# Top-k attention with an MLP behind it on one core: the opening loads, the place of the scores and the spread of the weight pieces

## The chip, the cores and the metric

The kernel runs on one core of a Trainium2 chip. The core has a matrix engine (TensorE, "PE" in the profile; its weight loads are "PEld"), a vector engine (VectorE, "DVE"), an engine for activations (ScalarE, "ACT"), a general one (GpSimd, "POOL") and one that issues transfers (SyncE, "SP"). Each works through its own list of instructions in order and waits on semaphores for the others. The metric is the device time of one execution in microseconds (us), the median over several.

## The reference

What is computed, with 8 batches, 8 heads, 576 rows and heads of 64, and then an MLP from 512 to 2048 and back:

```python
scores = (1 / sqrt(64)) * q @ k.T                  # per batch and head, 576 x 576
kth    = the 32nd largest score of each row
attn   = exp(scores - max), where scores >= kth, else 0
attn   = attn / (sum(attn) + 1e-9)
x      = (attn @ v), heads side by side            # 4608 x 512
h      = x @ w_in                                  # 4608 x 2048
out    = (h * sigmoid(1.702 * h)) @ w_out          # 4608 x 512
```

All data is float32.

## The kernel before

**Tiles and slots.** Heads are taken in pairs, four pairs a batch. The 576 rows of a head are four tiles of 128 rows and an end of 64. A *slot* is one tile of rows for one pair (two heads, 128 x 576 scores each), or the ends of two pairs. There are 144 slots, 18 a batch; slots 0 to 3 are the first row tile of the four pairs of batch 0.

**What a slot goes through.** `load` brings q and k of a pair (two transfers of 128 KB each and one of 32 KB for the 64 end rows), with row 4p + t on partition p at place t. `prepare` turns them on TensorE, and ScalarE copies the result to SBUF (L201, L206, L208). `scores` multiplies (L231), and ScalarE copies the scores out (L238). `topk` finds the 32 largest of each row on VectorE: eight MAX8 (L247) and six MATCH_REPLACE8 (L250), fourteen operations in a fixed order. `bounds` (GpSimd, L266, L267) takes the 32nd and the largest, `exponentials` (ScalarE, L275 a Prelu, L277 the exponentials with their sums) makes the unnormalised weights. `divide` inverts the sums on VectorE (L286, L288) and, in slots below SETTLED = 9, makes a diagonal matrix of them on GpSimd (L292), by which `turn` transposes and divides in one matmul (L308, L311); later slots divide on ScalarE and GpSimd (L294, L295). `values` multiplies by v (L338) into xT (L350). Once the four pairs of a row tile are there, `hidden` (L381), `tanh` (L398), `gate` (L411, L412, L414) and `project` (L429) do the MLP on it in four parts.

**Weights in pieces.** w_in and w_out are brought in 32 pieces of 128 x 512 float32 outputs, from raw transfers of 512 KB (L122), and `round_piece` splits the work on each: "size" on ScalarE (L144), "shift" on VectorE (L145), "low" and "sign" on ScalarE (L147, L146), "finish", two operations on GpSimd (L140, L141). `by_slot` says how many pieces each of slots 0 to 9 handles; the transfers of slot n's pieces are queued in slot n - 1, and eight raw buffers exist, each free when its piece is finished.

**The order.** It is written out by hand, in the order of the calls: `opening`, then `slot(n)` for n = 0 to 9, then `two_slots(n)`, which interleaves two slots. Every engine keeps this order. In `slot(n)` come the exponentials of slot n - 1, sizes, the preparing and scoring of slot n + 2, the top-k of slot n with the division of n - 1 after its sixth operation (i == 5), the shifts, and then turning and values of n - 1. Finishes not yet done wait in the list `unfinished`; a slot issues one after the third operation of its top-k and the others behind the division. `stay_warm` puts matmuls without a use on TensorE.

**Buffers and queues.** q and k of a pair lie in two buffers each, so pair 2 takes those of pair 0 once pair 0 has been turned. Scores have three buffers and the PSUM tiles for turning two. All transfers are issued by SP, in order; the order of the issues waits, for each transfer, for the one eight places before it, since eight completion semaphores go round.

Of the kernel before, what the change touches and what calls it, by code (L numbers as in the profile page):

```python
# [16 lines left out]
P = 128  # L17
# [11 lines left out]
def kernel(  # L29
# [6 lines left out]
    moe_w_out: bass.AP,  # L36
    out: bass.AP,
):

# [119 lines left out]
    def load(name, b, hp):  # L164
        src = q if name == "q" else k
        t = loads.tile([P, NF, 2, D], F32, name=f"{name}_l")
        for j in range(2):
            nc.sync.dma_start(t[:, :, j, :], src[b, 2 * hp + j, 0:FULL, :].rearrange("(p t) d -> p t d", t=NF))

        if name == "q":  # L170
            loaded["ends", b, hp] = loads.tile([P, 2, D], F32, name="ends")
        on = slice(0, TAIL) if name == "q" else slice(TAIL, P)
        nc.sync.dma_start(
            loaded["ends", b, hp][on, :, :], src[b, 2 * hp : 2 * hp + 2, FULL:S, :].rearrange("h p d -> p h d")
        )
        loaded[name, b, hp] = t

    def load_v(b, hp):
        main = vals.tile([P, 2, NF, D], F32, name="v_l")
        nc.sync.dma_start(  # L180
            main[:].rearrange("p j t d -> p j (t d)"),
            v[b, 2 * hp : 2 * hp + 2, 0:FULL, :].rearrange("j (p t) d -> p j (t d)", t=NF),
        )


        tail = v_ends[(b * NP + hp) % len(v_ends)]
        for j in range(2):
            nc.sync.dma_start(tail[j * TAIL : (j + 1) * TAIL, j, :], v[b, 2 * hp + j, FULL:S, :])
        vv[b, hp] = main, tail
# [138 lines left out]
    def values(n):  # L328
        b, t, hps = slots[n]
        pt = st[n]["pt"]  # L330
        outs = []
        for p in range(2 if t == NF else 1):
            cols = slice(p * TAIL, (p + 1) * TAIL) if t == NF else slice(0, P)
            main, tail = vv[b, hps[p]]
            o = ps_t.tile([P, 512], F32, name="o", tag="tp")
            for c in range(NF + 1):
                for j in range(2):
                    nc.tensor.matmul(  # L338
                        o[j * D : (j + 1) * D, 0 : cols.stop - cols.start],
                        lhsT=main[:, j, c, :] if c < NF else tail[:, j, :],  # L340
                        rhs=pt[:, j * NF + c if c < NF else 2 * NF, cols],
                        start=(c == 0),
                        stop=(c == NF),
                    )
            outs.append((o, hps[p]))
        for o, hp in outs:
            if t < NF:
                if (b, t) not in xts:
                    xts[b, t] = xtp.tile([P, CC, P], F32, name="xT")
                nc.scalar.copy(out=xts[b, t][:, hp, :], in_=o[:, 0:P])  # L350
            else:
                if (b // 2, t) not in xts:
                    xts[b // 2, t] = xtt.tile([P, CC, P], F32, name="xT_t")
                at = b % 2 * TAIL
                nc.scalar.copy(out=xts[b // 2, t][:, hp, at : at + TAIL], in_=o[:, 0:TAIL])
        if hps[-1] == NP - 1:
            if t < NF:
                to = out[b * S : b * S + FULL, :].rearrange("(p t) c -> p t c", t=NF)[:, t, :]
                ready.append((xts.pop((b, t)), [(slice(0, P), to)]))
            elif b % 2:  # L360
                first = [(b - 1 + i) * S + FULL for i in range(2)]
                rows = [(slice(i * TAIL, (i + 1) * TAIL), out[x : x + TAIL, :]) for i, x in enumerate(first)]
                ready.append((xts.pop((b // 2, t)), rows))
        st[n].clear()

# [53 lines left out]
    def project(blocks):  # L419
# [12 lines left out]
        if blocks[-1] == G - 1 and g == NG - 1:  # L432
            ob = osp.tile([P, C], F32, name="ob")
            nc.scalar.mul(out=ob[:], in_=po[:], mul=0.5 / RAISE**2)
            for on, to in rows:
                nc.sync.dma_start(to, ob[on, :])


    later = {}
# [7 lines left out]
    READY = (((-9, -8), (-7, -6), (-4, -3), (-2, -1)), ((-7, -6), (-4, -3), (-3, -2), (-1, -2)))  # L447
    FETCH = (((-13, -12), (-11, -10), (-7, -7), (-5, -4)), ((-11, -10), (-9, -8), (-5, -5), (-2, -2)))
    VALUES = ((-8, -7, 0, 0), (-8, -7, 2, 2))
    by_slot = dict(enumerate([2, 2, 3, 3, 3, 3, 4, 4, 4, 4]))  # L450
    for n in by_slot:
        first = sum(map(len, list(by_slot.values())[:n]))
        by_slot[n] = list(range(first, first + by_slot[n]))
    assert by_slot[len(by_slot) - 1][-1] == NPIECE - 1
    for n in range(2, len(by_slot)):
        for x in by_slot[n]:
            at(n - 1, load_piece, x)
        if n < NP + 1:
            at(n - 1, load_v, 0, n - 1)
    for hp in range(2, NP):  # L460
        for name in "qk":
            at(hp - 2, prepare, name, 0, hp)
    for b in range(1, B):
        for hp in range(NP):
            for i, name in enumerate("qk"):
# [2 lines left out]
            at(b * PER + VALUES[b % 2][hp], load_v, b, hp)  # L468
    unfinished = []

    early = []

    def opening():

        stay_warm(7, v_ends[0][:].rearrange("p j d -> p (j d)"))
        for hp in range(2):
            for name in "qk":
                load(name, 0, hp)
        for x in by_slot[0]:
            load_piece(x)  # L480
        for m in range(2):
            for name in "qk":
                prepare(name, 0, m)
            if m == 1:
                early.extend(round_piece(x) for x in by_slot[0])
                for piece in early:
                    piece["size"]()
            scores(m)
        for hp in range(2, NP):
            for name in "qk":  # L490
                load(name, 0, hp)
        load_v(0, 0)
        for x in by_slot[1]:
            load_piece(x)

    def slot(n):
        todo = later.pop(n, [])
# [7 lines left out]
        if before:  # L505
            bounds(n - 1)
            exponentials(n - 1)
        some = [round_piece(x) for x in by_slot.get(n, [])] if n else early
        if n == 0:
            for piece in some:  # L510
                piece["low"]()
                piece["sign"]()
        else:
            for piece in some[:2]:
                piece["size"]()
        if not settled:
            for args in preparing:
                prepare(*args)
            scores(n + 2)
            stay_warm(4)  # L520
        if n > 0:
            for piece in some[2:]:
                piece["size"]()
        tanh(aside)
        for i, op in enumerate(topk(n) if n < N else [lambda: None] * 14):
            op()
# [8 lines left out]
                gate(aside)  # L535
        for piece in some:
            piece["shift"]()
            unfinished.append(piece["finish"])
        if n == 0:
            return  # L540
        if aside:
# [1 line left out]
        if settled:  # L543
            for args in preparing[:1]:
                prepare(*args)
        for piece in some[:2]:
            piece["low"]()
        going = settled and len(to_project) > (2 if n < N else 0)
        if going:
            project(range(G - 1))  # L550
# [3 lines left out]
            project(range(G - 1, G))  # L554
        if before:
            turn_ends(n - 1)
        for piece in some[2:]:
            piece["low"]()
        if before:
            values(n - 1)  # L560
        for piece in some:
            piece["sign"]()
        if settled and n + 2 < N:
            scores(n + 2)
        if settled:
            for args in preparing[1:]:
                prepare(*args)
        if not ready and not settled:
            stay_warm(4)
        hidden()  # L570

    def two_slots(n):

# [23 lines left out]
        def find(m):  # L597
            for i, op in enumerate(topk(m) if live(m) else [lambda: None] * 14):
                op()
                if i == 5 and live(m - 1):  # L600
                    divide(m - 1)
                if i > 1 and unfinished:
                    unfinished.pop(0)()

        def middle(m):
# [74 lines left out]
```

## Time and profile before

| | before |
|---|---|
| time, median of 3 (lowest to highest) | 1630.75 us (1627.81 to 1632.36) |
| span of the profiled execution | 1630.6 us |
| TensorE busy | 1584.6 us, 97% |
| VectorE busy | 1479.2 us, 91% |
| ScalarE busy | 1155.9 us, 71% |
| GpSimd busy | 754.1 us, 46% |
| moved by DMA | 56.61 MB, mean 35 GB/s |

Busy shares are means over stages that differ: the first slots, in which the weights are still coming, have their own shares, and so has the end, where only the MLP is left. A row in order of time has its start, its length, the engine, the line, the operation with out<-in and, in square brackets, how long the engine stood idle before it and what ended that. A row "x3" merges three instructions, and its length is from the first one's start to the last one's end.

### The profile page before, as it was taken

The page shows a single profiled execution, that of the slowest core. Times are in us where ns is not written, and L with a number is a line of the kernel's source. Part 1 is how long each engine was busy: PE and PEld are TensorE (multiplying, and loading weights), DVE is VectorE, ACT ScalarE, POOL GpSimd, SP SyncE. Part 2 cuts the span into 40 slices and gives each one's busy share as a digit, 9 for nine tenths or more (in the row PEclk, how much of TensorE's full clock was granted, in tenths as well). Part 3 has the DMA queues.
Part 4 walks back from the last instruction along what each step waited for, and adds up shares of the span by engine and source line. Part 5 has one row for each costly group of instructions (what it writes and reads, how often), then busy time and mean ns, then how long its engine had stood idle before and what let it go on. Part 6 is the DMA issues. An engine that isn't in the chain of part 4 may idle for free.

```text
span 1630.6 us, 32137 instructions
## 1 busy us (share of the span) xinstructions
PE 1584.6 (97%) x12025; PEld 1184.1 (73%) x12025; DVE 1479.2 (91%) x3212; ACT 1155.9 (71%) x2449; POOL 754.1 (46%) x782
## 2 busy tenths in 40 slices
PE   7777999999999999999999999999999999999999
PEld 5665677777777777777777777777777777777776
DVE  6998999999999999999999998999999999999960
ACT  5896777777777776677777777777777777777761
POOL 2788344444444444444444444444444444444430
PEclk7898999999999999999999999999999999999999
DMA  7442001110001001110000100111000100000000
GB/s 209 124 137 76 22 22 29 30 43 16 22 15 44 22 23 29 29 37 22 22 15 23 35 17 15 30 30 44 15 22 15 43 22 23 22 8 7 8 8 14
DMA packets 100636, 56.61 MB, mean 35 GB/s; under 512 B 83584, under 2 KB 91776, under 8 KB 100480
## 3 DMA queue, kind: packets, MB, share of 16 engines
q1 hardware_dynamic: 100480, 54.55, 12.1%
q8 instruction: 95, 1.56, 0.4%
q14 instruction: 61, 0.50, 0.1%
HBM read 45.09 MB, written 9.44 MB: 33 GB/s over the span
## 4 chain that ended last, share of the span: by engine, by line
PE 88%; ACT 5%; DVE 4%; POOL 1%; issue 1%; SPq 0%; DMA 0%; POOLq 0%; ACTq 0%
PE ph L381 30%; PE po L429 29%; PE o L338 9%; PE s_ps L231 9%; PE tp L306 8%; DVE top L247 2%; DVE left L250 2%; PE tp L199 1%; ACT sc L238 1%; ACT pr L277 1%; ACT raw L146 1%; PE tp L308 1%; DVE wout L145 0%; ACT sc L275 0%; DMA raw<-in_moe_w_in_dram 0%
## 5 line engine op out<-in xcount | busy, mean ns | idle before, releaser
L247 DVE MAX8 top<-left 128x8 f32<-128x576 f32 x864 | 609.9, 747 | 0.0
L429 PE MATMUL po<-wout,gT 128*128 128x512 f32 x1152 | 542.1, 594 | 0.0
L381 PEld LDWEIGHTS ph<-xT,win 128*128 128x128 f32 x4096 | 467.5, 192 | 41.5 <-issue 40.8
L381 PE MATMUL ph<-xT,win 128*128 128x128 f32 x4096 | 484.6, 277 | 0.0
L250 DVE MATCH_REPLACE8 left<-top,left 128x576 f32<-128x576 f32 x576 | 423.4, 743 | 0.0
L295 POOL TENSOR_SCALAR pr<-pr,rden 128x576 f32<-128x576 f32 x135 | 233.4, 1729 | 356.0 <-ACT th L398 347.9
L411 POOL TENSOR_SCALAR th<-th 128x512 f32<-128x512 f32 x133 | 198.9, 1496 | 224.2 <-ACT th L398 224.2
L429 PEld LDWEIGHTS po<-wout,gT 128*128 128x128 f32 x1152 | 197.8, 191 | 142.3 <-issue 141.8
L275 ACT ACTIVATE sc<-sc,cut 128x576 f32<-128x576 f32 x288 | 208.1, 774 | 130.5 <-POOL cut L266 128.1
L316 ACT COPY pt<-tp 128x512 f32<-128x512 f32 (+1 forms) x432 | 193.2, 481 | 148.1 <-PE tp L306 141.0
L306 PEld LDWEIGHTS tp<-ident,pr 128*128 128x128 f32 x1215 | 145.7, 141 | 113.9 <-issue 65.8
L238 ACT COPY sc<-s_ps 128x576 f32<-128x576 f32 x288 | 169.9, 644 | 75.8 <-PE s_ps L231 75.4
L277 ACT ACTIVATE pr<-sc,low 128x576 f32<-128x576 f32 x288 | 219.2, 764 | 0.0
L247 DVE MAX8 top<-sc 128x8 f32<-128x576 f32 x288 | 202.2, 744 | 11.3 <-ACT sc L238 11.3
L250 DVE MATCH_REPLACE8 left<-top,sc 128x576 f32<-128x576 f32 x288 | 211.7, 743 | 0.0
L306 PE MATMUL tp<-ident,pr 128*128 128x128 f32 x1215 | 177.7, 273 | 9.0 <-ACT q_t L201 7.7
L231 PE MATMUL s_ps<-k_t,q_t 64*128 64x288 f32 (+1 forms) x1280 | 183.3, 433 | 0.9 <-ACT k_t L201 0.9
L412 POOL TENSOR_TENSOR gT<-th,h 128x512 f32<-128x512 f32 x133 | 169.8, 1277 | 11.1
L338 PE MATMUL o<-pt,v_l 128*64 128x128 f32 (+1 forms) x2560 | 158.9, 267 | 1.2 <-ACT pt L316 0.3
L338 PEld LDWEIGHTS o<-pt,v_l 128*64 128x64 f32 x2560 | 131.6, 138 | 31.3 <-ACT pt L316 15.8
L231 PEld LDWEIGHTS s_ps<-k_t,q_t 64*128 64x128 f32 (+1 forms) x1280 | 100.0, 178 | 59.6 <-issue 40.5
L266 POOL TENSOR_SCALAR cut<-top 128x2 f32<-128x2 f32 x144 | 38.2, 265 | 208.5 <-DVE top L247 206.8
(55 smaller groups left out, 1175.3 us busy)
## 6 DMA issues: line engine op xcount, KB each, us to landing
q_l<-in_q_dram SPq DMA_DIRECT2D x64, 128.0 KB, 2.9
k_l<-in_k_dram SPq DMA_DIRECT2D x64, 128.0 KB, 2.9
raw<-in_moe_w_in_dram SPq DMA_DIRECT2D x16, 512.0 KB, 5.1
v_l<-in_v_dram SPq DMA_DIRECT2D x32, 256.0 KB, 3.0
raw<-in_moe_w_out_dram SPq DMA_DIRECT2D x16, 512.0 KB, 3.3
out_dram<-ob SPq DMA_DIRECT2D x32, 256.0 KB, 2.3
ends<-in_q_dram SPq DMA_DIRECT2D x32, 32.0 KB, 2.4
ends<-in_k_dram SPq DMA_DIRECT2D x32, 32.0 KB, 2.6
```

What stands on the lines that cost most here:

```text
L231: nc.tensor.matmul(ps[i][rows, c, 0:HALF], lhsT=qT[b, hps[p]][on, cols], rhs=kT[b, hps[p]][on, FIRST[i] + c * HALF : FIRST[i] + (c + 1) * ...
L247: nc.vector.max(top[:, i, 8 * r : 8 * r + 8], (left if r else sc)[:, i, :])
L250: nc.vector.match_replace(left[:, i, :], top[:, i, 8 * r : 8 * r + 8], (left if r else sc)[:, i, :], LOWEST)
L275: nc.scalar.activation(sc[:, i, :], sc[:, i, :], AF.Prelu, bias=cut[:, i : i + 1], alpha=HUGE)
L277: nc.scalar.activation(pr[:, i * S : (i + 1) * S], sc[:, i, :], AF.Exp, bias=low[:, i : i + 1], accum_out=den[:, i : i + 1],)
L295: nc.gpsimd.tensor_scalar(pr[:, S : 2 * S], pr[:, S : 2 * S], rden[:, 1:2], None, op0=ALU.mult)
L306: nc.tensor.transpose(tp[:, c * P : (c + 1) * P], pr[:, at], ident[:])
L316: nc.scalar.copy(out=to, in_=tp[:, 0 : blocks * P])
L338: nc.tensor.matmul(o[j * D : (j + 1) * D, 0 : cols.stop - cols.start], lhsT=main[:, j, c, :] if c < NF else tail[:, j, :], rhs=pt[:, j * N ...
L381: nc.tensor.matmul(ph[:, i, :], lhsT=win[:, c, f * P : (f + 1) * P], rhs=xT[:, c, :], start=(c == 0), stop=(c == CC - 1),)
L411: nc.gpsimd.tensor_scalar(th[:], th[:], 1.0, None, op0=ALU.add)
L429: nc.tensor.matmul(po[:], lhsT=gT[:, i, :], rhs=wout[:, f, :], start=(f == 0), stop=(f == FC - 1))
```

## The change

It has five parts.

1. *First pair.* `load_first` issues k of pair 0 from ScalarE's queue, and only the first 128 rows of q (both heads, 64 KB) with the ends from SP. `prepare_first` turns these, with the small copies on VectorE. The other 384 rows of q are loaded behind pair 1 and the first two weight pieces (`load_rest`), and turned in slot 0 (`prepare_rest`). For this a q tile has to be 128 rows that follow each other, so q, k, v and the output go from row 4p + t to row 128t + p on partition p; v is then brought by two transfers of 128 KB in place of one of 256 KB. The aim is an earlier first top-k.
2. *Fourth pair later.* In the opening, v of pair 0 and slot 1's pieces are loaded ahead of pair 3.
3. *Scores behind the values.* From slot 2 on, `scores(n + 2)` follows `values(n - 1)` in each slot (before, from slot 8 on only).
4. *Pieces.* `by_slot` goes from 2, 2, 3, 3, 3, 3, 4, 4, 4, 4 to 2, 3, 3, 4, 4, 3, 4, 4, 3, 2. Low, sign and finish of slot 0's pieces go to the end of slot 1, and those of slot 1's to the start of slot 2 (`split`). In `two_slots` finishes are issued behind the division, no longer ahead of it.
5. *Warming matmuls.* 5 in place of 7 at the start, 8 in slot 0, 16 in slots 1 to 3 and 6 in slots 4 to 6, in place of 4 at one or two places of each of slots 0 to 7.

```diff
 def load(name, b, hp):
-            nc.sync.dma_start(t[:, :, j, :], src[...].rearrange("(p t) d -> p t d", t=NF))
+            nc.sync.dma_start(t[:, :, j, :], src[...].rearrange("(t p) d -> p t d", p=P))
...
+    def load_first():
...
+        for j in range(2):
+            nc.scalar.dma_start(
+                loaded["k", 0, 0][:, :, j, :], k[0, j, 0:FULL, :].rearrange("(t p) d -> p t d", p=P)
+            )
+        nc.scalar.dma_start(ends[TAIL:P, :, :], k[0, 0:2, FULL:S, :].rearrange("h p d -> p h d"))
+        nc.sync.dma_start(loaded["q", 0, 0][:, 0, :, :], q[0, 0:2, 0:P, :].rearrange("h p d -> p h d"))
+        nc.sync.dma_start(ends[0:TAIL, :, :], q[0, 0:2, FULL:S, :].rearrange("h p d -> p h d"))
...
+    def load_rest():
+        for j in range(2):
+            nc.sync.dma_start(
+                loaded["q", 0, 0][:, 1:NF, j, :], q[0, j, P:FULL, :].rearrange("(t p) d -> p t d", p=P)
+            )
...
-    by_slot = dict(enumerate([2, 2, 3, 3, 3, 3, 4, 4, 4, 4]))
+    by_slot = dict(enumerate([2, 3, 3, 4, 4, 3, 4, 4, 3, 2]))
...
 def opening():
-        stay_warm(7, v_ends[0][:].rearrange("p j d -> p (j d)"))
-        for hp in range(2):
-            for name in "qk":
-                load(name, 0, hp)
+        load_first()
+        stay_warm(5, v_ends[0][:].rearrange("p j d -> p (j d)"))
+        for name in "qk":
+            load(name, 0, 1)
         for x in by_slot[0]:
             load_piece(x)
...
+        load_rest()
+        prepare_first()
+        scores(0)
+        for name in "qk":
+            prepare(name, 0, 1)
+        scores(1)
         for hp in range(2, NP):
             for name in "qk":
                 load(name, 0, hp)
-        load_v(0, 0)
-        for x in by_slot[1]:
-            load_piece(x)
+            if hp == 2:
+                load_v(0, 0)
+                for x in by_slot[1]:
+                    load_piece(x)
+    def split(pieces):
+        for piece in pieces:
+            piece["low"]()
+            piece["sign"]()
+            unfinished.append(piece["finish"])
...
 def slot(n):
-        if not settled:
-            for args in preparing:
-                prepare(*args)
-            scores(n + 2)
-            stay_warm(4)
+        if n < 2:
+            early[n] = some
+        elif n == 2:
+            split(early[1])
...
+        if n == 0:
+            prepare_rest()
+        if n < 2:
+            for name in "qk":
+                prepare(name, 0, n + 2)
+            scores(n + 2)
...
         if before:
             values(n - 1)
+        if n == 1:
+            split(early[0])
...
-        if settled and n + 2 < N:
+        if 1 < n and n + 2 < N:
             scores(n + 2)
...
         if not ready and not settled:
-            stay_warm(4)
+            stay_warm(16)
         hidden()
+        if NP <= n < PROJECTS:
+            stay_warm(6)
...
 def two_slots(n):
-                if i > 1 and unfinished:
+                if i > 5 and unfinished:
                     unfinished.pop(0)()
```

## The prediction

> **What bounds the kernel now.** I read the page's slices first, then the stretches, then who waited for whom on VectorE in the first 200 us, then the order of time of that part.
>
> The slices: each digit is the busy share of a fortieth (40.8 us).
>
> ```profile
> PE   7777999999999999999999999999999999999999
> DVE  6998999999999999999999998999999999999960
> ACT  5896777777777776677777777777777777777761
> PEclk7898999999999999999999999999999999999999
> ```
>
> The stretches: length, then busy time of TensorE, its weight loads, VectorE, ScalarE, GpSimd, then the granted clock, DMA share and GB/s.
>
> ```profile
> 20.00:30.00 10.00, 7.53 (x31) 6.07 (x32) 8.57 (x21) 7.05 (x19) 6.30 (x8) 0.67 0.88 301
> 80.00:90.00 10.00, 8.35 (x79) 7.14 (x79) 9.23 (x20) 9.46 (x20) 8.73 (x8) 1.00 0.33 106
> 150.00:170.00 20.00, 12.27 (x68) 7.79 (x68) 14.02 (x31) 8.34 (x17) 12.85 (x13) 0.74 0.10 27
> 300.00:400.00 100.00, 100.00 (x725) 74.87 (x724) 94.71 (x208) 73.07 (x159) 46.16 (x47) 1.00 0.11 27
> ```
>
> From about 170 us to the end TensorE has no gap, so the end is "the time at which TensorE becomes gapless, plus what it has left". The change does not alter that remaining work. Before 170 us nothing on TensorE sets the pace: slots 0 to 10 are paced by VectorE's top-k with ScalarE and GpSimd close to full. A gain or loss there reaches the end one for one. Where VectorE stood still in the first 200 us (total, times, longest), and two of the rows in order of time:
>
> ```profile
> DVE some L286 <- ACT pr L277: 13.5, 5, 5.2
> DVE top L247 <- ACT sc L238: 11.3, 2, 9.6
> ...
> 42.36 0.17 DVE L286 TENSOR_SCALAR some<-den 128x2 f32<-128x2 f32 x1 [5.18 <-ACT pr L277]
> 48.19 1.08 DVE L145 TENSOR_SCALAR win<-win 128x512 uint32<-128x512 uint32 x3
> 138.63 4.06 DVE L145 TENSOR_SCALAR wout<-wout 128x512 uint32<-128x512 uint32 x4
> 180.49 1.40 DVE L247 MAX8 top<-sc 128x8 f32<-128x576 f32 x2
> 190.40 1.40 DVE L247 MAX8 top<-sc 128x8 f32<-128x576 f32 x2
> ```
>
> An undisturbed slot is 9.9 us (180.49 to 190.40). VectorE wants the sums of the previous slot (L286) some 4.2 us into a slot. The starts of slots 0 to 10 are 10.6, 20.9, 33.0, 49.2, 61.3, 73.3, 86.5, 99.0, 113.6, 128.1 and 142.6. So 33 us of these 132 are over 9.9 a slot: weight shifts of 0.36 to 1.0 us each (20 in all), waits for sums and for the gate (9), the gate itself (0.6 each).
>
> **What the Trainium skill says.** "SBUF — State Buffer", section "Who interferes with whom": a VectorE tensor_scalar may run in a two-port mode, and then it and a GpSimd instruction exclude each other for a whole instruction. The trace agrees: the shift takes 0.36 us (48.19, GpSimd idle) and 1.0 us (138.63, GpSimd busy with 1.3 us steps of finish). "DMA: Bandwidth & Descriptors", section "Issuing engines are not separate DMA queues": a second issuing engine saves issue time only, the 16 DMA engines being the same. Fits: early loads are issued every 0.65 us at 146 to 149 GB/s and a DMA share of 0.65, so issue is the limit there. "TensorE: Matmul & The Clock Gate", Part 1: the array runs at half clock after some 3.4 us of idling. The clock was 0.50 at 20 to 24 and 30 to 34 us, where eight score matmuls took 2.5 us against 1.24.
>
> **First pair.** Before, k's second half is issued at 3.46 and landed at 6.32; scores start at 7.77, top-k at 10.61. After, ScalarE issues k at 0.7 to 2.0 while SP issues 64 KB of q. With 2.9 us from issue to landing plus some sharing, k is there at 4.5; transposes 0.6, copy 0.7, scores at 5.9. From scores to the first maximum took 2.84 at half clock, about 1.6 at full: 7.6 to 8.8, I take 8.3. Gain 2.3 us at slot 0. Slot 0 ends at 8.3 + 9.7 + 0.7 (two shifts) = 18.7.
>
> **What eats it: the rest of q stands behind two weight pieces.** Pair 2 takes pair 0's q buffer, so its first load waits for the transposes of q's rest. Raw pieces are issued at 6.0 and 6.5. Before, pieces issued at 8.80 and 9.43 landed at 13.82 and 15.13, the loads just behind 0.5 us apart. Moved to the earlier issue: 11.0, 12.3, rest of q at 13.2. Transposes to 13.7; only then SP issues pair 2 (before at 9.98), six issues of 0.63, its last k at 16.25, landing 2.7 later: 19.0. Behind it on SP stand v, three pieces and pair 3. Pair 2's k copied by 20.1, scores (half clock) and the score copies to 23.6. Before, these ended at 22.45 + 1.18 = 23.63, because two pieces' low and sign (2.4 us, now moved behind) held the copies. So the same instant. The ScalarE queue has these copies ahead of slot 0's Prelu and exponentials (3.1 us); sums at 26.5 to 26.7, as before (26.51). VectorE waits 3.6 us where it waited 1.39: the gain of 2.3 is gone.
>
> **Pair 3 later.** Its loads now stand behind v and three pieces: pieces land at 24.6, 25.8, 27.1 (1.27 us each), pair 3 at 27.7 to 29.7; before 21.11. On ScalarE its copies come ahead of slot 3's score copies, the three sizes, the turning of slot 0, and then low and sign of the first two pieces: copies to 31.1, scores and copies to 34.0 (32.8 at full clock), sizes 35.7, turning and xT 38.5, split 40.9, then Prelu and exponentials of slot 1 to 44.1, against 42.36 before. Shifts of slot 1 wait for the sizes, slot 2 starts at 36 (33.0 before), and its wait for sums is 4 us (5.18 before).
>
> **Pieces.** All of 32 stay; each costs ScalarE 1.75, GpSimd 2.6 and VectorE 0.36 to 1.0. Their places go from 2,2,3,3,3,3,4,4,4,4 to 2,3,3,4,4,3,4,4,3,2. In slot 2 GpSimd gets the finishes of slots 0 and 1 together, five: after its diagonal at 45.6, four times 2.65 = 56.2, and the bounds of slot 2 stand behind them. Slot 2's top-k ends at 50.0, three slow shifts: slot 3 at 53 (49.2). Bounds 56.9, sums 60.0, wanted at 57.2: 2.8 us of waiting. Then 5.9 and 2.2 of shifts: slot 4 at 68 (61.3). Slot 4, four pieces over a busy GpSimd: 9.9 + 3.9, slot 5 at 82 (73.3). That is 8.7 us behind, with 16 pieces done instead of 13. Slots 5 to 9, each 9.9 + gate 0.6 + shifts (3 x 1.0; 1.0 + 3 x 0.36 and a little; 3.4; 3.0; 1.0), give 95.5, 108, 122, 135.5 and 147 (142.6 before): the smaller slots 8 and 9 and the missing waits for the gate return 4.3.
>
> **Scores behind the values** move 1.1 us of score copies, with no work added; four sizes then reach the gate's tanh without them, which removes waits of 0.55 to 0.77 in three slots (counted above). Scores have a full slot until they are wanted. **Warming matmuls** sit after the scores, where TensorE waits for GpSimd's diagonal: 16 pairs are about 4 us at full clock in a gap of 7. Nothing. **Row order** of q, k, v and out: q and k moved in 256 B runs before too. Only v goes from 1 KB to 256 B runs and from one issue to two, 0.6 us of SP each, counted in the opening; later DMA is at 0.1.
>
> **Slot 10.** Before, GpSimd ran finishes for 10.4 us, division 1.7, gate 2.8 and so came to slot 10's bounds 15.15 after the slot's start. TensorE stood 7.73 us at 154.8 and then had clock 0.50 until about 168. After: the division comes first (at +4.5), then two finishes 5.3, gate 2.8, bounds at +14.3, so the next copy that TensorE needs is at +19.5 instead of +19.95: 0.5 gained. TensorE has been busy longer by then (idle from about +15.1, 4.4 us), so the half-clock stretch, worth up to 2.5 us (5 us at 0.50), may shrink: I take half, 1.2. Sum: +4.4 - 0.5 - 1.2 = +2.7, so 1630.75 + 2.7 = 1633.5. Bounds: if pair 2 and 3 come 1.5 us earlier and no half clock, +0; if every early piece meets GpSimd, +7.
>
> **Rivals.**
> (a) Faster, 0.24: the early delays are smaller than I walk them. Start 2.3 gained and kept, slot 1's 1.39 gone, slot 2's 5.18 halved (2.6), slots 8 and 9 with three shifts of 1.0 fewer (3), slot 10 with 1.7; against it three more shifts in slots 1, 3 and 4 and a wait of slot 3 (4). Net 7.0: 1624. For it: ScalarE has the low and sign steps off its path at the start. Against: pair 2's load hangs behind the pieces.
> (b) Slower, 0.32: the queue of finishes in slot 2 carries on through slots 3 and 4, every shift there at 1.0 (2.6 more), ScalarE's four-piece slot of 12.5 us then makes slot 7 wait 1 to 2 for sums, and no clock is won in slot 10 (1.2): +2.7 + 5.3 = 1639. For it: GpSimd was busy 8.73 of 10 at 80 to 90 us, ScalarE 9.46. Against: slots 3 and 4 before ran with GpSimd full and lost only 2.0 each.
> (c) TensorE hides the opening, as its total is fixed: 1631. Included in my forecast's band; against it, TensorE's idle time lies all before 170 us.
>
> **How the numbers follow.** Forecast, no change that a measurement tells (within 4.9 us): 0.44, at 1633.5. Faster 0.24, slower 0.32. The range takes in most of both rivals' spread of some 2 us about 1624 and 1639: 1622 to 1641.
>
> **What would show it.** Right: top-k starts near 8.3 yet slot 0's sums come near 26.5; the first load of pair 2 starts only when q's rest is transposed, near 13.7; slot 5 starts later than 73.3; shifts of slots 3 and 4 over 0.5 us each; slot 10 within 4 us of 147. Wrong: sums of slot 0 before 24, or slot 5 at or before 76, or TensorE's gap in slot 10 gone, each of which points to (a); slot 5 after 85 to (b).

## The result, and the profile after

| | before | after |
|---|---|---|
| time, median (lowest to highest, 4 runs each) | 1630.38 us (1627.81 to 1632.36) | 1637.91 us (1636.19 to 1638.47) |
| span of the profiled execution | 1630.6 us | 1635.9 us |
| TensorE, VectorE busy | 1584.6, 1479.2 us | 1590.3, 1488.6 us |
| ScalarE, GpSimd busy | 1155.9, 754.1 us | 1156.3, 751.1 us |

The ratio is 1.0045, with a 95% interval of 1.0028 to 1.0063: 7.5 us slower, which is more than the 4.9 us that the prediction named as the bound of a change that can be told. So the outcome that it held most likely, no change (0.44), did not come; the slower one (0.32) did. The forecast of 1633.5 was 4.4 us too low; the time lies in its range and beside rival (b), 1639.

Most lines stand 35 to 37 further down than before, those of `round_piece` 3 further up. L286 (the sums on VectorE) is now L323, the shift L145 is L142, the finish L140 and L141 is L137 and L138, the bounds L266 are L303, the division on GpSimd L295 is L332, the gate L411 and L412 is L446 and L447.

The slices of the page of after, as shown of before:

```profile
PE   7779899999999999999999999999999999999999
DVE  6999899999999999999999998999999999999960
ACT  5886776777777777777777777677777777777761
PEclk9899999999999999999999999999999999999999
```

The same four stretches of after (length, TensorE, weight loads, VectorE, ScalarE, GpSimd, clock, DMA share, GB/s):

```profile
20.00:30.00 10.00, 5.75 (x33) 4.32 (x33) 9.85 (x22) 5.39 (x14) 1.42 (x5) 0.83 0.99 264
80.00:90.00 10.00, 6.90 (x70) 6.17 (x70) 9.97 (x24) 8.71 (x18) 7.98 (x10) 1.00 0.31 108
150.00:170.00 20.00, 14.37 (x76) 10.08 (x76) 16.41 (x39) 9.40 (x20) 12.86 (x12) 0.91 0.00 0
300.00:400.00 100.00, 100.00 (x761) 75.91 (x758) 94.72 (x205) 71.91 (x153) 45.02 (x48) 1.00 0.15 36
```

At 300 to 400 us TensorE has no gap in either kernel. So the difference is made earlier, as the prediction took it. VectorE is busy almost without a break at 20 to 30 and at 80 to 90 us (9.85 and 9.97 of 10), where before it waited (8.57 and 9.23). At 80 to 90 us this is no gain: a shift that is held up counts as busy. At 20 to 30 us it has no shift, and no wait for slot 0's sums; but GpSimd has next to nothing to do there (1.42 against 6.30), and that work comes later.

Who VectorE waited for in the first 200 us of after (total, times, longest):

```profile
DVE some L323 <- ACT pr L314: 11.0, 5, 3.9
...
DVE top L284 <- ACT sc L275: 4.0, 2, 2.4
DVE win L142 <- ACT win L141: 1.5, 1, 1.5
...
DVE gT L449 <- ACT th L433: 0.3, 1, 0.3
```

Waits for sums (first row) fell from 13.5 to 11.0 and those for the gate (last row) from 2.1 to 0.3; the row of before for the gate is

```profile
DVE gT L414 <- ACT th L398: 2.1, 3, 0.8
```

What rose is the time of the shifts. Two of their rows in order of time, with the arrival of slot 1's sums ahead of them:

```profile
40.97 0.17 DVE L323 TENSOR_SCALAR some<-den 128x2 f32<-128x2 f32 x1 [3.88 <-ACT pr L314]
...
46.81 4.29 DVE L142 TENSOR_SCALAR win<-win 128x512 uint32<-128x512 uint32 x3
...
62.68 3.56 DVE L142 TENSOR_SCALAR win<-win 128x512 uint32<-128x512 uint32 x4
```

The three shifts of slot 2 took 4.29 us from the first's start to the last's end; the same three before took 1.08 (the row at 48.19 in the prediction). The starts of the slots (first MAX8 of each), in us:

| slot | 0 | 2 | 3 | 4 | 5 | 8 | 10 | 12 | 14 |
|---|---|---|---|---|---|---|---|---|---|
| before | 10.6 | 33.0 | 49.2 | 61.3 | 73.3 | 113.6 | 142.6 | 168.6 | 190.4 |
| predicted | 8.3 | 36 | 53 | 68 | 82 | 122 | 147 | | |
| after | 9.6 | 32.9 | 51.0 | 66.2 | 80.6 | 123.1 | 148.8 | 173.9 | 195.5 |

Slot 10 starts 6.2 us later. Taken apart over slots 0 to 9: the start itself -1.0; the shifts, each time from the first one's start to the next slot, 29.2 against 20.0 (+9.3); a wait of slot 1's first shift for its size +1.5; waits for sums 5.8 against 7.3 (-1.5); waits for the gate 0.3 against 2.1 (-1.8); the rest -0.3. From slot 14 on 5.1 us are left, and the spans differ by 5.3.

### The profile page after: what moved, and what is told of

Its sections match the earlier page's. It is cut to its first block, busy times and chain, and to the rows that moved or that the text cites. A ratio compares the mean times of both kernels' runs of the same rounds, so it can differ in the third digit from the quotient of the medians.

```text
span 1635.9 us, 32268 instructions
## 1 busy us (share of the span) xinstructions
PE 1590.3 (97%) x12081; PEld 1190.4 (73%) x12081; DVE 1488.6 (91%) x3216; ACT 1156.3 (71%) x2446; POOL 751.1 (46%) x782
## 4 chain that ended last, share of the span: by engine, by line
PE 87%; DVE 7%; ACT 3%; POOL 1%; issue 1%; DMA 1%; SPq 0%; ACTq 0%; POOLq 0%
PE ph L416 30%; PE po L464 29%; PE s_ps L268 9%; PE o L375 9%; PE tp L343 8%; DVE top L284 3%; DVE left L287 2%; PE tp L236 1%; DVE wout L142 1%; ACT sc L275 1%; ACT pr L314 1%; DMA k_l<-in_k_dram 1%; DVE win L142 0%; PE tp L345 0%; POOL win L137 0%
## 5 line engine op out<-in xcount | busy, mean ns | idle before, releaser
L332 POOL TENSOR_SCALAR pr<-pr,rden 128x576 f32<-128x576 f32 x135 | 233.1, 1727 | 361.1 <-ACT th L433 348.2
L446 POOL TENSOR_SCALAR th<-th 128x512 f32<-128x512 f32 x133 | 198.8, 1494 | 224.3 <-ACT th L433 224.3
L447 POOL TENSOR_TENSOR gT<-th,h 128x512 f32<-128x512 f32 x133 | 169.6, 1276 | 11.1
L303 POOL TENSOR_SCALAR cut<-top 128x2 f32<-128x2 f32 x144 | 35.3, 245 | 207.6 <-DVE top L284 207.6
```

Source lines behind the costliest of these rows:

```text
L332: nc.gpsimd.tensor_scalar(pr[:, S : 2 * S], pr[:, S : 2 * S], rden[:, 1:2], None, op0=ALU.mult)
L446: nc.gpsimd.tensor_scalar(th[:], th[:], 1.0, None, op0=ALU.add)
```

## Experiments

Each of the twelve kernels that follow was timed beside the kernel before, whose median was then between 1629.8 and 1630.9 us; the row of after has the runs above. Summary, in the order of the argument (S5 and S10 are the starts of slots 5 and 10, "11" the length of slot 11, all in us from one profile each; with the same old opening, slot 0 starts anywhere from 9.6 to 11.2 in five profiles, so 1 us in S5 or S10 says little):

| kernel | what it is | median | ratio (95%) | S5 | S10 | 11 |
|---|---|---|---|---|---|---|
| after | the change | 1637.91 | 1.0045 (1.0028 to 1.0063) | 80.6 | 148.8 | 15.2 |
| a_i1 | after, finishes in two_slots as before | 1630.86 | 1.0000 (0.9992 to 1.0008) | 80.4 | 148.1 | 10.3 |
| a_own_i1 | and low, sign, finish of slots 0 and 1 in their own slots | 1627.07 | 0.9980 (0.9972 to 0.9988) | 76.7 | 144.5 | 10.3 |
| a_split_early | after, slot 0's low and sign early in slot 1 | 1634.51 | 1.0020 (1.0012 to 1.0028) | 78.6 | 146.8 | 15.2 |
| a_old_spread | after, by_slot of before | 1635.05 | 1.0031 (1.0022 to 1.0040) | 71.2 | 141.0 | 20.4 |
| b_new_spread | before, by_slot of after | 1627.14 | 0.9976 (0.9966 to 0.9986) | 76.9 | 144.2 | 10.3 |
| b_spread_scores | and scores behind the values | 1628.30 | 0.9988 (0.9982 to 0.9995) | 77.5 | 145.3 | 10.3 |
| b_opening | before, opening of after | 1631.04 | 0.9999 (0.9990 to 1.0007) | 73.7 | 143.1 | 16.0 |
| b_diag_act | b_new_spread, diagonal on ScalarE, finishes first | 1633.04 | 1.0013 (1.0005 to 1.0021) | 78.0 | 149.3 | 10.3 |
| a_own_diag_act | the same on a_own_i1 | 1629.97 | 1.0001 (0.9992 to 1.0009) | 77.5 | 147.9 | 10.2 |
| b_two_first | b_new_spread, two finishes ahead of the division | 1622.89 | 0.9950 (0.9936 to 0.9963) | 78.8 | 142.0 | 10.3 |
| b_two_open | and the opening of after | 1622.62 | 0.9955 (0.9942 to 0.9967) | 77.1 | 139.1 | 10.3 |
| a_own_two | a_own_i1, two finishes ahead of the division | 1620.88 | 0.9943 (0.9930 to 0.9957) | 74.2 | 137.9 | 10.3 |

### Where the finishes of the last slots stand

a_i1:

```diff
 def two_slots(n):
-                if i > 5 and unfinished:
+                if i > 1 and unfinished:
```

> The changed kernel with one number put back: in the two-slot stage finishes are issued from the third operation of the top-k on (i > 1) and no longer only behind the division (i > 5). Theory F (with two pieces left, finishes ahead of the division would fit into GpSimd's idle time at the start of slot 10, and behind it they hold up slot 10's bounds): slot 10 starts as before at 148.8, slot 11 lasts 10 to 11 us instead of 15.2, slot 12 starts at 169 to 170 instead of 173.9, time 1633 to 1634. Rival: TensorE hides it, as it is gapless from there on: 1637 to 1638.

One number gives back as much as the whole change lost: 1630.86 for 1637.91, a larger step than the expected one to 1633 or 1634. The start of slot 10 is hardly moved (148.1 for 148.8), so nearly all of this arises behind it. GpSimd in slot 10 of after, in order of time:

```profile
148.59 0.34 POOL L304 TENSOR_TENSOR low<-top 128x2 f32<-128x2 f32 x1
153.42 1.72 POOL L332 TENSOR_SCALAR pr<-pr,rden 128x576 f32<-128x576 f32 x1 [4.49 <-DVE rden L325]
155.11 1.29 POOL L137 TENSOR_TENSOR wout<-wout,raw 128x512 int32<-128x512 int32 x1
...
161.93 1.26 POOL L447 TENSOR_TENSOR gT<-th,h 128x512 f32<-128x512 f32 x1
163.16 0.23 POOL L303 TENSOR_SCALAR cut<-top 128x2 f32<-128x2 f32 x1
```

and of a_i1:

```profile
147.90 0.34 POOL L304 TENSOR_TENSOR low<-top 128x2 f32<-128x2 f32 x1
148.19 1.29 POOL L137 TENSOR_TENSOR wout<-wout,raw 128x512 int32<-128x512 int32 x1
...
153.48 1.72 POOL L332 TENSOR_SCALAR pr<-pr,rden 128x576 f32<-128x576 f32 x1
...
158.19 0.23 POOL L303 TENSOR_SCALAR cut<-top 128x2 f32<-128x2 f32 x1 [0.17 <-DVE top L284]
```

With `i > 5`, GpSimd stands idle 4.49 us until VectorE has inverted the sums, and only then does the two finishes, 5.2 us, ahead of the gate and of slot 10's bounds. With `i > 1` the same two finishes fill just that gap: the division is as early (153.48 and 153.42), and the bounds come at 158.19 in place of 163.16, 4.97 us earlier. Slot 11 falls from 15.2 us to 10.25, slot 12 from 11.7 to 9.9; together they give 6.8 of the 7.05 us between the two medians.

That is more than the bounds explain: counted from the start of slot 10 they come 4.3 us earlier. The rest agrees with TensorE's clock. TensorE waits there for the next q, and these are the rows behind that wait, of after and then of a_i1:

```profile
167.87 1.11 PE L343 MATMUL tp<-ident,pr 128*128 128x128 f32 x4 [5.63 <-ACT q_t L238]
```

```profile
162.99 0.63 PE L343 MATMUL tp<-ident,pr 128*128 128x128 f32 x4 [1.45 <-ACT q_t L238]
```

and the same stretch of both, in the columns of the stretches above:

```profile
167.00:173.00 6.00, 5.13 (x15) 2.67 (x15) 5.32 (x11) 3.31 (x7) 4.80 (x5) 0.50 0.13 44
```

```profile
167.00:173.00 6.00, 6.00 (x48) 5.38 (x48) 5.97 (x15) 5.02 (x12) 0.47 (x3) 1.00 0.18 42
```

After its 5.63 us of idling TensorE has a clock of 0.50, from 167.9 to 173.3 us; after 1.45 us it keeps 1.00. An estimate from these figures: 5.4 us at half clock are 2.7 us of lost work, and 4.3 + 2.7 = 7.0. The two parts were not tried one without the other.

### The spread of the pieces

b_new_spread, one line of the kernel before, and a_old_spread, the reverse in the kernel after:

```diff
-    by_slot = dict(enumerate([2, 2, 3, 3, 3, 3, 4, 4, 4, 4]))
+    by_slot = dict(enumerate([2, 3, 3, 4, 4, 3, 4, 4, 3, 2]))
```

> The kernel before with only the new number of pieces a slot (2, 3, 3, 4, 4, 3, 4, 4, 3, 2). Theory S: slot 5 at 78 or later (73.3 before), slot 10 at 145 to 146 (142.6 before), time 1633 to 1634. Theory G: slot 5 about 76, paid back in slots 8 and 9, slot 10 at 141 to 143, time 1629 to 1631.

> The changed kernel with the pieces of before (2, 2, 3, 3, 3, 3, 4, 4, 4, 4). Theory S: slot 5 near 74, slot 10 near 143, time 1631 to 1632. Theory G: slot 5 near 76 to 77, since four finishes still come together in slot 2 and start only at 36; slots 8 and 9 then carry four pieces, so slot 10 at 147 or later and time 1637 to 1639.

Alone, the new spread makes the kernel before 3.6 us faster, where neither theory had a time below 1629. Slot 10 starts 1.6 us later (144.2 for 142.6), since more pieces are handled in slots 3 and 4, where shifts meet finishes (3.5 and 4.6 us of shifts for 2.0 each); but slots 10 and 11 take 21.3 us in place of 26.0, as GpSimd has two finishes left there and no longer four. In after the old spread brings slot 5 to 71.2 and slot 10 to 141.0 instead of 148.8, earlier than either theory had it, and slot 11 then takes 20.4 us, with 8.7 us of waiting for sums: four finishes stand behind the division. The interval overlaps with that of after, so under `i > 5` and the late split the two spreads are not told apart. The spread and `i > 5` both act on slots 10 and 11: in the kernel before the new spread takes 4.6 us off these two, and `i > 5` puts about as much back.

### When the first pieces are split

a_split_early calls `split(early[0])` right behind the exponentials of slot 0, at the start of slot 1:

```diff
             early[n] = some
+        if n == 1:
+            split(early[0])
         elif n == 2:
             split(early[1])
...
-        if n == 1:
-            split(early[0])
-        else:
+        if n != 1:
             for piece in some:
```

> The changed kernel, with low and sign of slot 0's two pieces right behind slot 0's exponentials (start of slot 1) instead of at the end of slot 1. Theory G (GpSimd's finishes come too late and pile up: first one at 36.5 us against 21.2 before, five in slot 2, and VectorE's shifts wait behind them): first finish at about 26, three finishes in slot 2, slot 2's shifts 2 to 3 us instead of 4.2, slot 5 starts 3 to 4 us earlier (77 instead of 80.6), slot 10 2 to 4 earlier (145 to 147), time 1634 to 1636. Theory S (the loss is four pieces instead of three in slots 3 and 4): slot 10 within 1 us of 148.8, time 1637 to 1638.

It gains 3.4 us on after, as expected, though the intervals of the two ratios touch. GpSimd's first finish begins at 23.50 where in after it had to wait for ScalarE's sign step:

```profile
36.48 1.31 POOL L137 TENSOR_TENSOR win<-win,raw 128x512 int32<-128x512 int32 x1 [6.12 <-ACT raw L144]
```

Slot 2 falls from 18.1 us to 12.0 (its three shifts from 4.2 to 1.0), but slot 3 rises from 15.1 to 18.9 with a wait of 5.4 us for sums: part of the piled-up work only moves one slot on. a_own_i1 avoids the pile. On top of a_i1, slot 0's pieces get their low and sign in slot 0, behind their sizes, and their finishes in slot 1; slot 1's pieces go the way of all later ones:

```diff
-        if n < 2:
-            early[n] = some
-        elif n == 2:
-            split(early[1])
...
+        if n == 0:
+            split(some)
...
-        if n > 1:
+        if n > 0:
             for piece in some[:2]:
...
-        if n == 1:
-            split(early[0])
-        else:
-            for piece in some:
-                piece["sign"]()
-                unfinished.append(piece["finish"])
+        for piece in some:
+            piece["sign"]()
+            unfinished.append(piece["finish"])
```

> The changed kernel without two of its edits: finishes in the two-slot stage as before (i > 1), and low, sign and finish of the pieces of slots 0 and 1 in their own slots as before. The opening, scores behind the values, the new number of pieces and the warming matmuls stay. If these two edits are the whole loss: slot 2's shifts near 2 us, slot 10 at 143 to 145, slot 12 at 164 to 166, time 1626 to 1628. If the scores, the warming or the opening cost something too: slot 10 at 146 or later, time 1630 or more.

Against a_i1 this is 3.8 us faster, and slot 5 starts 3.7 us earlier (76.7 for 80.4), slot 10 3.6 (144.5 for 148.1): the gain is made in slots 1 to 4. Not all of it is seen to reach the end: slot 10 takes 11.1 us in place of 9.9, with a wait of 0.9 for sums, and from slot 11 on 2.5 us are left in the two profiles, whose spans differ by 2.5 too. With it, the changed kernel is 0.2% faster than the one before.

The ratios now make a chain from before to after: the new spread 0.9976, with the opening, the scores and the warming matmuls 0.9980 (a_own_i1), with the late split 1.0000 (a_i1), with `i > 5` 1.0045. In us of the medians: -3.6, -0.1, +3.8, +7.0, together 7.1 of the 7.5 measured. The second step also holds what the list of five parts does not name: in slots 1 to 3, v is queued ahead of the pieces. The prices are those of this order of the edits. a_old_spread splits late as well and yet starts slot 10 at 141.0, earlier than before (142.6); with two pieces in slot 1 and not three, the late split is not seen to cost anything ahead of slot 10.

### The opening, and the scores behind the values

b_opening gives the kernel before the first pair from two queues, the row order and pair 3 behind v and slot 1's pieces; the pieces keep their places and work. b_spread_scores moves the scores from slot 2 on behind the values in b_new_spread:

```diff
             for args in preparing:
                 prepare(*args)
-            scores(n + 2)
+            if n < 2:
+                scores(n + 2)
             stay_warm(4)
...
-        if settled and n + 2 < N:
+        if 1 < n and n + 2 < N:
             scores(n + 2)
```

> The kernel before with the opening alone: first pair from two queues, q in two steps, row order, pair 3 behind v and slot 1's pieces; pieces, scores, warming matmuls, finishes as before (low and sign of slot 0's pieces in slot 0). If the opening is worth something by itself: top-k starts at 9.6 instead of 10.6, sums of slot 1 at 40.5 to 42 instead of 42.4, slot 10 at 141 to 142, time 1629 to 1630. If later pair 3 loads cost more than that: slot 2's wait for sums over 5.2 us, slot 10 at 144 or later, time 1632 or more.

> The kernel before with the new number of pieces and with scores behind the values from slot 2 on, nothing else. If the place of the scores matters: the waits for the gate (1.7 us in slots 6 and 7) go away and slot 10 starts 1 to 2 us earlier than the 144.2 of the new number alone, time 1625 to 1626.5. If not: 1627 within 1, or later if TensorE comes late to the scores.

The opening is worth nothing that can be told: 0.9999 (0.9990 to 1.0007), with a time between the two that were expected. Slot 0 starts at 9.4, and slot 1 waits 3.17 us for sums where it waited 1.39; slot 2 starts at 33.6 (33.0 before). Scores behind the values take the waits for the gate down from 1.7 to 0.2 us, and the median is 1.2 us up on b_new_spread (0.9988 for 0.9976, the intervals just overlap): no gain in any case.

### GpSimd relieved in two ways

b_diag_act takes the diagonal to ScalarE and lets all finishes run after the third operation of the top-k; a_own_diag_act is the same edit on a_own_i1:

```diff
-                nc.gpsimd.tensor_scalar(by[:, i, :], ident[:], rden[:, i : i + 1], None, op0=ALU.mult)
+                nc.scalar.activation(by[:, i, :], ident[:], AF.Copy, scale=rden[:, i : i + 1])
...
-            if i == 2 and unfinished:
-                unfinished.pop(0)()
-            if i == 5:
-                if before:
-                    divide(n - 1)
+            if i == 2:
                 while unfinished:
                     unfinished.pop(0)()
+            if i == 5 and before:
+                divide(n - 1)
```

> The kernel before with the new number of pieces and the diagonal of slots 0 to 8 made on ScalarE, so that GpSimd issues all finishes from the third top-k operation on. Theory G2 (in slots 3 to 8 GpSimd's own order sets the slot: bounds 1.0, one finish 2.6, idle 1.9 until the division, diagonal 1.2, three finishes 7.8, together 14.5, and VectorE's shifts wait behind the last finishes): slots 3 to 8 last 12 to 13.3 us instead of 12.3 to 15.1, shifts at most half, slot 10 at 134 to 139 instead of 144.2, time 1618 to 1623. Rival (ScalarE is as full, and the 0.5 us more and the later diagonal cost what GpSimd saves): slot 10 at 143 or later, time 1627 to 1630.

> The same two edits (diagonal on ScalarE, all finishes from the third operation on) in the changed kernel with its two costly edits put back. Theory G2: slot 10 at 134 to 139 instead of 144.5, time 1618 to 1623; with scores behind the values ScalarE reaches the diagonal about 1 us earlier than in the other, so no later than that. Rival: 1627 or more.

The shifts did what was hoped: in b_diag_act they take 10.6 us in slots 0 to 9, 0.33 us each, as this row of slot 2 shows, with the row of waits over the first 200 us behind it:

```profile
47.10 1.08 DVE L145 TENSOR_SCALAR win<-win 128x512 uint32<-128x512 uint32 x3
```

```profile
DVE some L286 <- ACT pr L277: 20.0, 8, 4.0
```

But waits for sums are 20.0 us where b_new_spread has 7.4, and the kernel is 5.9 us slower than b_new_spread; a_own_diag_act is 2.9 us slower than a_own_i1. Slot 10 was expected at 134 to 139 and came at 149.3 and 147.9. ScalarE makes the sums, and the two diagonal copies (0.69 us in all) stand in its list too; which of the two edits holds the sums up more was not taken apart. Short shifts are thus no gain where the sums come later for it.

b_two_first goes half way: two finishes ahead of the division, the rest behind, the diagonal left on GpSimd.

```diff
-            if i == 2 and unfinished:
-                unfinished.pop(0)()
+            if i == 2:
+                for _ in range(min(2, len(unfinished))):
+                    unfinished.pop(0)()
```

> The kernel before with the new number of pieces and two finishes, not one, issued ahead of the division (third top-k operation); the diagonal stays on GpSimd. Theory G2: GpSimd's idle 1.9 us before the diagonal are filled, so four-piece followers shorten by up to 1.9 us each, slot 10 at 138 to 141, time 1622 to 1625. Rival (the diagonal 1.7 us later holds up turning, and with it ScalarE and the sums): slot 10 at 144 or later, time 1627 or more.

It takes 4.3 us off b_new_spread, within the time expected, though slot 10 (142.0) came later than the 138 to 141 expected. GpSimd in slot 5 of b_new_spread and of b_two_first (the diagonal with the idle time ahead of it, and the last finish of the slot):

```profile
81.53 1.18 POOL L292 TENSOR_SCALAR by<-ident,rden 128x128 f32<-128x128 f32 x2 [1.88 <-DVE rden L288]
...
89.51 1.35 POOL L141 TENSOR_TENSOR win<-win,raw 128x512 f32<-128x512 f32 x1
```

```profile
83.40 1.18 POOL L292 TENSOR_SCALAR by<-ident,rden 128x128 f32<-128x128 f32 x2 [0.76 <-DVE rden L288]
...
88.56 1.30 POOL L141 TENSOR_TENSOR win<-win,raw 128x512 f32<-128x512 f32 x1
```

and the three shifts of that slot on VectorE, of b_new_spread and then of b_two_first:

```profile
87.42 3.73 DVE L145 TENSOR_SCALAR wout<-wout 128x512 uint32<-128x512 uint32 x3
```

```profile
89.28 1.52 DVE L145 TENSOR_SCALAR wout<-wout 128x512 uint32<-128x512 uint32 x3
```

The slot of b_two_first started 1.87 us later (78.78 for 76.91), so its shifts begin 10.5 us into the slot in both. There the last finish of b_two_first has 0.6 us left to run (to 89.86), and that of b_new_spread 3.4 (to 90.86): of the three shifts one waits, in place of all three. Shifts over slots 0 to 9 total 15.4 us.

The last two put the parts together. b_two_open is b_two_first with the opening of b_opening, a_own_two is a_own_i1 with the edit of b_two_first:

> The kernel before with the new spread, two finishes ahead of the division, and the opening of the change (first pair from two queues, row order, fourth pair later); scores stay ahead of the top-k up to slot 7. Theory (the opening is worth nothing, since slot 1 waits for sums by what slot 0 gained): within 1.5 us of the same kernel without the opening, 1622.9, so 1622 to 1624, slot 1 waiting 3 us or more for sums. Rival (slot 1's wait can be used, as pair 2 lands earlier): 1620 to 1621.

> The changed kernel with finishes of two_slots again from the third operation on, low/sign/finish of slots 0 and 1 in their own slots, and two finishes ahead of the division in slots 3 to 9. Theory (shifts of a slot meet fewer GpSimd finishes when two of them are done while VectorE is still in its top-k): as it took 4.3 us off the kernel before with the new spread, it takes 3 to 5 us off 1627: 1622 to 1624, with shifts under 18 us in slots 0 to 9 (26.9 without) and slot 10 starting near 141. Rival (scores behind the values leave GpSimd and ScalarE a tighter order, and the two finishes only delay the diagonal): 1626 to 1628, with waits for sums up by as much as shifts go down.

b_two_open takes 1622.62 (1622.33 to 1623.28), as b_two_first; so the opening again gives nothing, though slot 1 waits 1.75 us for sums there and not the 3 expected. a_own_two, which has every part of the change but the late split and `i > 5`, and two finishes first, takes 1620.88 (1619.85 to 1621.37 over five runs, below the 1622 to 1624 expected and below all runs of b_two_open). It beats both kernels: 0.9943 (0.9930 to 0.9957) of before. Its shifts take 15.1 us, its waits for sums 8.4, and slot 10 starts at 137.9.

## Why the prediction was right or wrong

**What bounds the kernel: right.** From the start of slot 14 to the end of the span it is 1440.2 us in before (1630.6 - 190.4), 1440.3 in after (1635.9 - 195.5), and between these two in a_i1, a_own_i1, b_new_spread, b_opening, b_two_first and a_own_two. What is lost or won ahead of it reaches the end one for one.

**First pair: the sum right, the reason wrong.** Slot 0 was to start at 8.3 and started at 9.6, and as predicted nothing of the gain is left at slot 2 (32.9 for 33.0). k landed by 4.4 and its transposes began at 4.48, as walked; the scores began at 6.57 where 5.9 was predicted, and took 2.67 us. That is about as long as the 2.50 us of before at a recorded clock of 0.50; in after the profile records no clock below 1.00 there, so the half clock is not shown. The gain was to be eaten by a wait of 3.6 us for slot 0's sums. In after there is no such wait; slot 1's first shift waits for its size instead, which ScalarE makes behind pair 3's copies:

```profile
23.98 0.16 DVE L323 TENSOR_SCALAR some<-den 128x2 f32<-128x2 f32 x1
...
31.43 1.55 DVE L142 TENSOR_SCALAR win<-win 128x512 uint32<-128x512 uint32 x3 [1.55 <-ACT win L141]
```

The wait for sums is found in b_opening, where ScalarE does low and sign of slot 0's pieces ahead of pair 2's copies, as before:

```profile
27.11 0.17 DVE L323 TENSOR_SCALAR some<-den 128x2 f32<-128x2 f32 x1 [3.17 <-ACT pr L314]
```

**"Pair 2 takes pair 0's q buffer, so its first load waits for the transposes of q's rest": wrong.** The first load of pair 2 on SP's queue:

```profile
10.32 0.92 SPq L165 DMA_DIRECT2D q_l<-in_q_dram  x2
```

and the matmuls that free the two q buffers, L236 those of pair 1 and L212 those of the rest of pair 0:

```profile
9.18 1.11 PE L236 MATMUL tp<-ident,q_l 128*128 128x128 f32 x4
...
14.26 0.90 PE L212 MATMUL tp<-ident,q_l 128*128 128x128 f32 x3
```

The load went out 0.03 us after pair 1's transposes ended (10.29) and 3.9 ahead of L212, where the prediction had 13.7: the profile names pair 1's transposes as what ended its wait. So it took pair 1's buffer, which in the order of the program is given back first. Pair 2 was there at 15.5 (19.0 predicted), pair 3 at 26.3 (29.7), slot 0's sums by 24.0 without a wait (26.5), slot 1's at 41.0 (44.1). So slot 2 started 3 us earlier than walked.

**Pieces: the mechanism right, the size of the shifts wrong.** Five finishes do meet in slot 2, and slot 3 does wait for sums (1.65 us, 2.8 predicted). But for slots 2 to 9 the prediction sums its shifts to 3.0 + 2.2 + 3.9 in slots 2 to 4 and 12.5 in slots 5 to 9, 21.6 us; 27.1 were measured. It took 1.0 us for a shift beside GpSimd and 0.36 for those it thought free. With finishes back to back a shift takes 1.1 to 1.4 (4.29 for the three of slot 2, 3.6 for the three of slots 5 and 8), and fewer were free: slot 3 took 3.5 for 2.2, slot 6 2.9 for 2.1. The two errors, -3 us at the start of slot 2 and +5 from there to slot 10, nearly cancel and leave slot 10 at 148.8 for 147. That it came so close is luck.

**Late split: not costed as an edit of its own, and it should have been.** Moving low, sign and finish back a slot was walked only inside the times above. With the new spread it costs 3.8 us (a_i1 against a_own_i1).

**Slot 10: the bounds right, the clock wrong, the parts hidden.** The division was predicted at +4.5 and the bounds at +14.3; they came at +4.6 and +14.4. TensorE's wait was put at 4.4 us and was 5.6. From slot 10 to the end the gain was put at 1.7 us, 0.5 for the bounds and 1.2 for a shorter stretch at half clock, and was 0.9 to 1.1. The bounds gave 0.8 of it (+14.4 for +15.15). The clock gave next to nothing: that its mean at 150 to 170 us is 0.91 for 0.74 misleads, as the wait ends 5.3 us later in after. TensorE works at 0.50 from 162.6 to 168.4 us in before and from 167.9 to 173.3 in after.

All this is the net of two edits of opposite sign: fewer pieces bring the bounds to +10.1 (a_i1), and `i > 5` puts 4.3 us back. Had each been priced by itself, 7 us would have stood against the change. The step "the division comes first, then two finishes" was summed correctly and failed in what it was compared with: the two finishes fit into the 4.49 us for which GpSimd stands idle ahead of that division.

**Scores behind the values, row order: right** that they bring nothing (b_spread_scores, b_opening). The 16 and 6 warming matmuls were not tried alone; b_spread_scores and a_own_i1 differ by them, by the opening and by how the first pieces are placed, and overlap (0.9988 and 0.9980).

**The rivals.** (b) named the carried-on queue of finishes and fast shifts turned slow, and that is what happened in slots 2 to 8; that no clock is won in slot 10 came true as well. The wait in slot 7 did not: it was 0.3 us and not 1 to 2. (a) failed at slot 5, which started at 80.6, far from its 76, though slot 0's sums came as early as its sign "before 24". (c) is left without support: what changes ahead of slot 14 reaches the end. Two of the signs for the forecast failed (slot 0's sums near 26.5, the first load of pair 2 near 13.7), while slot 5, the shifts of slots 3 and 4 and slot 10 were as it said. In all, the slots account for 5 us of the 7.5. The profiled run of before, 1632.4 us, was the slowest of its four; it is 5.2 us from the profiled run of after (1637.6), where the medians differ by 7.5.

## What to carry to other kernels

Price each edit by itself, above all where two of them touch one stretch: here a gain of 3.6 us (pieces spread away from the critical slot) and losses of 3.8 (the late split) and 7 (work moved behind a wait) were to make one number that looked like "nothing". A price can depend on the other edits, as that of the late split did on the spread. An engine that works in order and waits for a small result can be given filler that ends just before the result comes. None of it ahead of the wait was worse here (`i > 5`: 4.5 us idle, then late), and two finishes ahead of each division made the best version. All of it ahead was only tried together with the diagonal on ScalarE (b_diag_act), and lost. Before a transfer is said to wait for a buffer, look up which of the pool's buffers is given back first in the order of the program.

## What the runs showed of the hardware

- A shift (tensor_scalar, 128 x 512 uint32) takes 0.33 us with no finish in its way and up to 1.5 among finishes whose two steps take 1.3 us each, as if it waited for a whole step; the first step of a finish among shifts takes 1.48 in place of 1.30 (87.95 us in b_new_spread). It goes the other way too: at 48.19 us of before, where the prediction took GpSimd to be idle, the first of the bounds, 0.22 us elsewhere (29.98 us in after), takes 0.98 beside the three shifts. This agrees with the Trainium skill, "SBUF — State Buffer", section "Who interferes with whom", which tells of full exclusion and not of sharing. MAX8 and MATCH_REPLACE8 take 0.74 to 0.75 us on the mean, whether GpSimd works all through them or not at all.
- The eight first score matmuls took 2.50 us in the profile of before (recorded clock 0.50) and 1.46 in that of b_new_spread (1.00), whose opening is the same, and slot 0 started at 10.6 and 9.55; in b_two_first at 11.2. "TensorE: Matmul & The Clock Gate", Part 1, says that the window in which activity is watched runs freely, so that the same kernel has a different number of slow matmuls from one execution to the next; these numbers agree. A microsecond at the start of one profile is therefore no evidence on the opening. Taken together the profiles do show a difference: 9.35 to 9.85 us in the nine with the new opening, 9.55 to 11.22 in the five with the old.
